# Casts of wo behind the second tile's exponentials, last output copies first and through the tail buffers, the first x block in two pairs of tiles, x stores moved

## The chip, the cores and the metric

The kernel runs on one core of a Trainium2 chip. The metric is the device time of one execution in microseconds (us). The kernel before was run three times: 1636.6, 1637.58 and 1639.58 us, so its median is 1637.58 us. The engines are called as the profile calls them: PE (matmuls), ACT (ScalarE), DVE (VectorE), POOL (GpSimd) and SP (the queue that issues most transfers).

## The reference

A layer norm without weights, a linear attention A on the normalised rows, and a gated feed-forward network B on the same rows, whose product is added to the input:

```python
x = A_x                                   # 1 x 2048 x 576
xn = _layernorm(x)
qkv = xn @ wqkv                           # 32 heads of 18
pq, pk = per-head q @ w_phi, k @ w_phi
phi_q = concat(softmax(pq), softmax(-pq)) # and phi_k likewise
kv = einsum("bhsf,bhsd->bhfd", phi_k, v); z = sum of phi_k over s
o = (phi_q @ kv) / (phi_q . z + 1e-6)
s = o @ wo
g = silu((silu(xn @ w_gate) * (xn @ w_up)) @ w_down)   # 576 -> 4608 -> 576
out = x + s * g
```

## The kernel before, in words

**Stages.** All matmuls take float32 values in split form: a rounded high part and a remainder (`split`: an ACT copy and a DVE subtraction, L58 and L59). First the rows are loaded in blocks of 512 (four tiles `xn` of 128 rows), normalised, transposed on PE and split into the resident tiles `X` (`norm_stats`, `norm_block`, to about 75 us). Then come the k and v products, softmaxes and sums of the attention (the kv stage, to about 229 us), then the q stage (to about 486 us): eight steps of two `q_tile`s (softmax features of q), `numer` (their product with the summed k and v) and `project` (the product with `wo`, held as `WOH` and `WOL`). `project` fills a PSUM tile `ps` of 128x288 with 15 matmuls (L614), ACT copies it to `so` (L619) and stores it to `s_dram`. From 512.6 us on runs the feed-forward network (FFN), to the end.

**FFN.** `w_gate` and `w_up` are cut into 36 blocks of 128 columns. Five of them ("early", `early_tile`, PSUM `pe`, ACT silu L119, DVE product L122) are worked off between the matmuls of the attention and straight ahead of the FFN; their result goes to `h_dram`. The other 31 are units that `gate_up_weights` fetches: a load `ld` (L676), four POOL subtractions into `ts` and `ld` (L694 to L697), splits into `w`, stores of the split weights to `w_dram` for the second half of the rows, and one load `wt` from `t_dram` (L692). A unit is seven products of seven matmuls each into the PSUM banks `px` (two buffers), `py`, `pw` and one half of `pd`; between its products ACT copies `px` into `py` (L761) and takes snapshots `s` of `px` (L736), which PE's next product into the same bank waits for. The down products (`pd`, L832) follow as fill-in from the second pair of blocks on; their weights are `dw`, made from the rows `rt`, `rb` or `acc` and POOL's differences `td` (L917 to L924).

**Tails.** The last 64 of the 576 rows of each `w_gate` and `w_up` block don't fill a matmul, so they are prepared apart, by `tails(n)` (L541 to L554), eight times for four blocks each: a load into `tl` (two buffers, L544), four POOL subtractions in `tl` (L546 to L549), an ACT cast into `th` (one buffer, L550), a DVE subtraction (L551), and twelve stores to `t_dram` issued by POOL (eight of `th`, four of `tl`, L554). A unit's `wt` load reads what its tail has stored. `tl` and `th` lie in the pool `qk` of the q stage.

**What sets the order.** The program is written once; a scheduler orders each engine's queue from priorities and estimated times. `issue_after` adds an edge within one engine. Buffers of a pool are handed out in the order in which the program asks for them: who asks later for the same slot waits for the earlier user. Each engine works through its queue in the order that results. In the source the tails are asked for after all steps of the q stage, each behind one of the q tiles' last products (`last_e`). `keep_x` (L301) stores three `X` tiles to `a_dram`; `split_wo` is asked for after the first two q tiles and stands behind `read[-1]`, DVE's last subtraction of the second one.

Of the kernel before, what the change touches and what calls it, by code (L numbers as in the profile page):

```python
# [9 lines left out]
F32 = mybir.dt.float32  # L10
F32R = mybir.dt.float32r
AF = mybir.ActivationFunctionType
ALU = mybir.AluOpType
# [4 lines left out]
P = 128  # L18
NT = S // P
BT = 512  # L20
# [3 lines left out]
HALF = D // 2  # L24
# [22 lines left out]
def gated_hedgehog_kernel(ctx: ExitStack, tc, x, w_qk, w_v, w_phi, wo, w_gu, w_tail, w_down, ident_in, mask_in, out):  # L47
# [65 lines left out]
    def early_tile(f, i, parts, js=(0, 1), banks=None):  # L113
# [10 lines left out]
        return last  # L124

    with ExitStack() as att:
        const = att.enter_context(tc.tile_pool(name="const", bufs=1))
# [8 lines left out]
        with ExitStack() as wst:  # L136
# [4 lines left out]
            with ExitStack() as pst:  # L141
# [17 lines left out]

                def norm_stats(bs, xns):  # L160
                    t = slice(4 * bs[0], 4 * bs[-1] + 4)
                    for i, xn in zip(range(t.start, t.stop), xns):
                        for k in range(2):
                            nc.vector.bn_stats(stats[:, i, k, :], xn[:, k * HALF:(k + 1) * HALF])
# [8 lines left out]
                    return nc.vector.scalar_tensor_tensor(q, mv[:, t, 0], -1.0, r, op0=ALU.mult, op1=ALU.mult)  # L173

                def norm_block(b, xns):
                    for n, (i, xn) in enumerate(zip(range(4 * b, 4 * b + 4), xns)):
                        if n % 2:
                            nc.scalar.activation(xn[:, 0:D], xn[:, 0:D], AF.Identity, bias=rt[:, i:i + 1],
                                                 scale=rs[:, i:i + 1])
                        else:  # L180
                            nc.vector.tensor_scalar(xn[:, 0:D], xn[:, 0:D], mv[:, i, 0:1], rs[:, i:i + 1],
                                                    op0=ALU.subtract, op1=ALU.mult)
                        for k in range(2):
                            nc.gpsimd.tensor_copy(xn[:, D + k * P:D + (k + 1) * P].rearrange("p (j n) -> p j n", j=4),
                                                  xn[:, 512 + 32 * k:544 + 32 * k].unsqueeze(1).to_broadcast([P, 4, 32]))
                    i, j = divmod(b, 2)
                    dst = XB[i][2 * j:2 * j + 2]
                    for c in range(3):
                        ps = pps.tile([P, 2, BT], F32, name="tp", bufs=3)
                        for m in range(2):  # L190
                            o = (2 * c + m) * P if c < 2 else D + m * P
                            for n in range(4):
                                nc.tensor.transpose(ps[:, m, n * P:(n + 1) * P], xns[n][:, o:o + P], ident)
                        if c < 2:
                            nc.scalar.copy(dst[c][:, 0:2], ps)
                            nc.vector.tensor_sub(dst[c][:, 3:5], ps, dst[c][:, 0:2])
                            continue
                        xr = prep.tile([P, 2, BT], F32, name="xr", bufs=1)
                        for m in range(2):
                            nc.scalar.copy(dst[m][:, 2], ps[:, m])  # L200
                        nc.scalar.copy(xr, ps)
                        for m in range(2):
                            nc.gpsimd.tensor_sub(dst[m][32:64, 2], xr[32:64, m], dst[m][32:64, 2])
                            nc.scalar.dma_start(x_dram[i, :, :, 2 * j + m].rearrange("s p n -> p s n"),
                                                xr[:, m].rearrange("p (s n) -> p s n", s=4))

                def load_fold(m):
# [46 lines left out]
                wq = load_fold(1)  # L254
                norm_stats([0, 1], xns)
                norm_block(0, xns[0:4])
# [16 lines left out]
            def softmax_parts(ps, e):  # L273
# [7 lines left out]
                for s in range(2):  # L281
                    nc.scalar.activation(e[:, s * D:(s + 1) * D], e[:, s * D:(s + 1) * D], AF.Exp,
                                         scale=1.0 if s == 0 else -1.0)
# [4 lines left out]
            kk_pool, read = kk, []  # L288

# [29 lines left out]
            def sum_parts(k):  # L319
                r = raws[k]  # L320
                lo = los[k] = kk.tile([P, 4, 2, P], F32R, name="slo", bufs=1)
                for a in (2, 0):
# [5 lines left out]
                    nc.sync.dma_start(sum_dram[k // 4, :, j, k % 4, 0:3], hi.bitcast(F32))  # L328
                    nc.sync.dma_start(sum_dram[k // 4, :, j, k % 4, 3:5], lo[:, j].bitcast(F32))

# [97 lines left out]
            for p in range(8):  # L428
# [93 lines left out]
        with ExitStack() as qst:  # L522
# [75 lines left out]
            def project(b, oh, ol, last):  # L598
                for j in range(QS // P):
# [3 lines left out]
                    for i in range(2):  # L603
# [8 lines left out]
                        for g, (o, w) in enumerate(GROUPS):  # L612
                            for a, bw in ((oh, WOH), (oh, WOL), (ol, WOH)):
                                nc.tensor.matmul(ps[:, 0:HALF], a[0:w, g, jc], bw[0:w, g, n], start=k == 0,  # L614
                                                 stop=k == 3 * NG - 1)
                                k += 1
                        so = qk.tile([P, HALF], F32, name="so", bufs=2)
                        with tc.high_priority() if last else ExitStack():
                            nc.scalar.copy(so, ps[:, 0:HALF])  # L619
                        nc.scalar.dma_start(s_dram[r0:r0 + P, n], so)  # L620
# [408 lines left out]
    early_tile(EARLY - 1, 0, parts)  # L1029
    ready = [gate_up_weights(*todo.pop(0))]  # L1030
    est.close()
# [74 lines left out]
```

## Time and profile before

| | |
|---|---|
| median of the runs | 1637.58 us (1636.6 to 1639.58) |
| the profiled execution | 1638.38 us, its span 1636.6 us, 25198 instructions |
| mean granted TensorE clock | 0.998 |
| PE busy | 1604.0 us, 98% of the span, 9385 matmuls |
| DVE, ACT, POOL busy | 1168.5, 721.9, 653.3 us |
| first FFN matmul | at 512.60 us |
| tails in the trace | first cast at 251.2, last at 420.2 us; stores from 253.0 to 430.3 us |

A row of the timeline gives the start, the duration, engine, line, operation, out<-in and count of a run of like instructions; in brackets stands the idle time of the engine ahead of it and what ended it. A row of the groups gives minimum, median and maximum of the duration of one instruction in ns. A row of the table by windows gives the window, its length and for each engine the busy time with the number of instructions, then the granted clock of PE, the share of the DMA engines and GB/s. A row of PE's waits gives who waited for what, the sum in us, how often, and the longest. A row of the DMA issues gives the transfer, its queue, count, size, and the median us from issue to landing.

### The profile page before, as it was taken

Reading aid. Unit: us, or ns where it says so; the run is one execution under the profiler, and the core shown is the slowest. Engines: PE = TensorE matmul, PEld = TensorE weight load, DVE = VectorE, ACT = ScalarE, POOL = GpSimd, SP = SyncE. Lnnn points to the kernel's source line nnn. Section 1 sums busy time; section 2 is a strip of 40 time slices with the busy share of each in tenths; the row PEclk is TensorE's granted clock in tenths of the full one; section 3 lists DMA queues with packets and bytes.
Section 4 is the critical chain, followed back from the end, with each engine's and each line's share of the span. In section 5 each row is a group of like instructions: output and inputs, shape, how many; then the busy total and the mean of one; then the engine's idle time right before and its main releaser. Section 6 shows DMA issues by size and latency. Waiting matters only on the chain.

```text
span 1636.6 us, 25198 instructions
## 1 busy us (share of the span) xinstructions
PE 1604.0 (98%) x9385; PEld 1429.7 (87%) x9385; DVE 1168.5 (71%) x1721; ACT 721.9 (44%) x1391; POOL 653.3 (40%) x699
## 2 busy tenths in 40 slices
PE   6999998999999999999999999999999999999998
PEld 5899997999978888888888888888888888888887
DVE  7677768899952678778777778825666766666578
ACT  5533345444432554544444544455433433333334
POOL 3485661333212455455545355313233324133132
PEclk9999999999999999999999999999999999999999
DMA  9622243334248545555554554684454655555444
GB/s 286 206 80 78 85 134 117 117 103 126 67 144 306 184 165 175 179 178 168 177 180 165 175 192 152 224 296 150 136 162 135 199 184 170 172 179 185 140 115 174
DMA packets 121741, 268.46 MB, mean 164 GB/s; under 512 B 12787, under 2 KB 53363, under 8 KB 119827
## 3 DMA queue, kind: packets, MB, share of 16 engines
q1 hardware_dynamic: 106652, 246.49, 45.9%
q0 software_dynamic: 3072, 11.02, 2.4%
q10 hardware_dynamic: 11894, 9.35, 1.8%
q8 instruction: 74, 1.21, 0.3%
q14 instruction: 49, 0.39, 0.1%
HBM read 167.19 MB, written 99.61 MB: 163 GB/s over the span
## 4 chain that ended last, share of the span: by engine, by line
PE 90%; DMA 4%; DVE 3%; POOL 1%; issue 1%; ACT 1%; SPq 0%; ACTq 0%; POOLq 0%; DVEq 0%
PE px L707 24%; PE pd L832 24%; PE pw L707 12%; PE py L707 6%; PE p L92 6%; PE pe L92 5%; PE p L614 4%; PE po L594 2%; PE kvp L294 2%; PE vx L382 1%; PE pt L588 1%; DMA xn<-in_A_x 1%; PE vw L382 1%; DMA s_dram<-so 1%; DMA sraw<-in_A_w_v 1%
## 5 line engine op out<-in xcount | busy, mean ns | idle before, releaser
L832 PEld LDWEIGHTS pd<-dw,hh 128*128 128x128 f32 x3048 | 432.4, 188 | 26.4 <-DVE dw L59 1.7
L832 PE MATMUL pd<-dw,hh 128*128 128x288 f32 x3048 | 448.5, 297 | 4.3 <-DVE dw L59 1.5
L707 PE MATMUL px<-X,w 128*128 128x512 f32 x1488 | 384.3, 393 | 0.0
L707 PEld LDWEIGHTS px<-X,w 128*128 128x128 f32 x1488 | 270.6, 188 | 51.8 <-ACT s L736 2.0
L707 PE MATMUL pw<-X,w 128*128 128x512 f32 x732 | 188.7, 393 | 0.0
L707 PEld LDWEIGHTS pw<-X,w 128*128 128x128 f32 x732 | 137.0, 188 | 30.5
L741 DVE TENSOR_TENSOR s<-pw,s 128x512 f32<-128x512 f32 x124 | 85.1, 688 | 100.0 <-ACT s L736 89.2
L957 DVE TENSOR_TENSOR acc<-pd,acc 128x576 f32<-128x576 f32 x128 | 96.2, 752 | 83.8 <-PE pd L832 83.6
L736 ACT COPY s<-px 128x512 f32<-128x512 f32 x124 | 72.6, 585 | 157.2 <-PE px L707 157.2
L92 PE MATMUL pe<-X,wh 128*128 128x512 f32 (+1 forms) x380 | 121.8, 401 | 5.8 <-ACT h L119 2.9
L59 DVE TENSOR_TENSOR hh<-ha,hh 128x512 fp32r<-128x512 f32 x140 | 111.5, 823 | 20.7 <-ACT hh L58 19.1
L58 ACT CAST hh<-ha 128x512 fp32r<-128x512 f32 x140 | 82.7, 619 | 92.4 <-PE pd L832 73.5
L929 POOL TENSOR_TENSOR hb<-hb 128x512 f32<-128x512 f32 x34 | 47.0, 1381 | 168.6 <-DVE hb L753 161.4
L59 DVE TENSOR_TENSOR w<-ld,w 128x512 fp32r<-128x512 f32 (+1 forms) x93 | 77.2, 832 | 35.7 <-ACT w L58 34.5
L707 PE MATMUL px<-X,wt 96*128 96x512 f32 x248 | 97.9, 395 | 0.0
L707 PE MATMUL py<-X,w 128*128 128x512 f32 x372 | 96.5, 394 | 0.0
L916 POOL TENSOR_TENSOR h<-ha,hb 128x512 f32<-128x512 f32 x34 | 44.3, 1302 | 126.8 <-DVE ha L757 88.6
L942 POOL TENSOR_TENSOR ha<-ha 128x512 f32<-128x512 f32 x34 | 52.6, 1564 | 103.5 <-DVE hh L59 103.5
L58 ACT CAST w<-ld 128x512 fp32r<-128x512 f32 (+1 forms) x93 | 51.0, 549 | 89.6 <-POOL ld L697 56.8
L92 PEld LDWEIGHTS pe<-X,wh 128*128 128x128 f32 (+1 forms) x380 | 70.0, 189 | 21.7 <-ACT h L119 3.4
L761 ACT COPY py<-px 128x512 f32<-128x512 f32 x62 | 35.5, 572 | 102.7 <-PE px L707 80.8
L707 PEld LDWEIGHTS py<-X,w 128*128 128x128 f32 x372 | 66.7, 188 | 11.2
(262 smaller groups left out, 3199.0 us busy)
## 6 DMA issues: line engine op xcount, KB each, us to landing
w_dram<-w SPq DMA_DIRECT2D x90, 512.0 KB, 2.9
w<-w_dram SPq DMA_DIRECT2D x90, 512.0 KB, 4.5
wt<-t_dram SPq DMA_DIRECT2D x61, 336.0 KB, 3.7
ld<-in_B_w_gu SPq DMA_DIRECT2D x31, 512.0 KB, 4.5
X<-sum_dram SPq DMA_DIRECT2D x8, 1280.0 KB, 11.1
rt<-in_B_w_down SPq DMA_DIRECT2D x33, 288.0 KB, 3.1
rb<-in_B_w_down SPq DMA_DIRECT2D x33, 288.0 KB, 4.7
w_dram<-w SPq DMA_DIRECT2D x30, 256.0 KB, 2.1
```

The costliest lines, as they stand in the source:

```text
L58: nc.scalar.copy(hi, src)
L59: nc.vector.tensor_sub(lo, src, hi)
L92: last = nc.tensor.matmul(ps, l, r, start=n == 0, stop=n == len(pairs) - 1)
L614: nc.tensor.matmul(ps[:, 0:HALF], a[0:w, g, jc], bw[0:w, g, n], start=k == 0, stop=k == 3 * NG - 1)
L707: nc.tensor.matmul(ps, l, r, start=first and n == 0, stop=last and n == len(mm) - 1, skip_group_check=True)
L736: nc.scalar.copy(t, ps)
L741: nc.vector.tensor_add(t, ps, t)
L832: nc.tensor.matmul(ps, l, r, start=first and n == 0 and m == 0, stop=n == len(hs) - 1 and m == 2, skip_group_check=True)
L916: sub(s, g["h"][0][0], g["h"][0][1])
L929: nc.gpsimd.tensor_add(a21, a21, g["h"][1][1])
L942: sub(a12, a12, g["h"][0][0])
L957: nc.vector.tensor_add(a2, pd[:, :, 0:HALF], a2)
```

## The change

The first block of x is normalised and transposed in two pairs of tiles, and the next block's statistics stand behind the first block's last subtraction on DVE (`rest`) instead of behind its statistics. The stores of `keep_x` are issued behind the last store of that step's sums (`done`). The casts of `wo` stand behind the second tile's last exponential on ACT (`exps[-1]`), and the third `wo` buffer is a slot of `e` instead of `ez`. In the last step's second half (`last and i`) the output copies go to slots of `tl`, and the first unit's loads and weights (`gate_up_weights`) are issued behind the last output copy.

```diff
-                def norm_stats(bs, xns):
-                    t = slice(4 * bs[0], 4 * bs[-1] + 4)
+                def norm_stats(t, xns):
...
+                def turn(ps, c, ns, xns):
+                    for m in range(2):
+                        o = (2 * c + m) * P if c < 2 else D + m * P
+                        for n in ns:
+                            nc.tensor.transpose(ps[:, m, n * P:(n + 1) * P], xns[n][:, o:o + P], ident)
...
-                chain = norm_stats([2], xns[0:4])
-                norm_block(2, xns[0:4])
+                tps = [pps.tile([P, 2, BT], F32, name="tp", bufs=3) for _ in range(3)]
+                for n in (0, 2):
+                    norm_stats(slice(8 + n, 10 + n), xns[n:n + 2])
+                    norm_tiles(slice(8 + n, 10 + n), xns[n:n + 2])
+                    for c in range(3):
+                        turn(tps[c], c, (n, n + 1), xns)
+                rest = norm_block(2, xns[0:4], tps)
                 first_weights = [early_weights(0)]
-                with tc.issue_after(chain.ins):
-                    norm_stats([3], xns[4:8])
+                with tc.issue_after(rest.ins):
+                    norm_stats(slice(12, 16), xns[4:8])
...
-                sum_parts(order[p - 1])
+                done = sum_parts(order[p - 1])
                 load_stack(order[p])
                 if p == 3:
-                    keep_x()
+                    with tc.issue_after(done.ins):
+                        keep_x()
...
-                   qk.tile([P, 2, D], F32, name="ez", bufs=1)]
+                   qk.tile([P, 2 * D], F32, name="e", bufs=4).rearrange("p (a n) -> p a n", a=2)]
...
             def split_wo():
-                with tc.issue_after(read[-1].ins):
+                with tc.issue_after(exps[-1].ins):
...
-                        so = qk.tile([P, HALF], F32, name="so", bufs=2)
+                        if last and i:
+                            so = qk.tile([P, 7, P], F32, name="tl", bufs=2).rearrange("p a n -> p (a n)")[:, 0:HALF]
+                        else:
+                            so = qk.tile([P, HALF], F32, name="so", bufs=2)
                         with tc.high_priority() if last else ExitStack():
-                            nc.scalar.copy(so, ps[:, 0:HALF])
+                            outs.append(nc.scalar.copy(so, ps[:, 0:HALF]))
...
-    ready = [gate_up_weights(*todo.pop(0))]
+    with tc.issue_after(outs[-1].ins):
+        ready = [gate_up_weights(*todo.pop(0))]
```

The change has its effect through the order of the queues. On ACT, at the start of the q stage (exponentials L282 of the kernel before, L298 of the changed one; L58 the casts of `wo` out of the buffers `oh`, `ol` and `ez` or `e`), the kernel before has:

```order
L282 ACTIVATE e<-e 128x576 x2
L58 CAST WOH<-oh 126x1152
L58 CAST WOH<-ol 126x1152
L58 CAST WOH<-ez 72x576
L550 CAST th<-tl 128x896
L282 ACTIVATE e<-e 128x576
```

And the changed kernel, at the same place:

```order
L119 ACT_TABLE_LOAD
L119 ACTIVATE h<-pe 128x512
L298 ACT_TABLE_LOAD
L298 ACTIVATE e<-e 128x576 x2
L58 CAST WOH<-oh 126x1152
L58 CAST WOH<-ol 126x1152
L58 CAST WOH<-e 72x576
```

The three casts have moved behind the second tile's two exponentials, and the cast of the first tail (L550) has left this place.

On ACT, from the early tiles' silus to the first snapshots of the FFN, the kernel before has (L119 an early tile's silu, L761 the copy of `px` into `py`, L736 a snapshot):

```order
L119 ACTIVATE h<-pe 128x512
L62 CAST wh<-raw 128x768
L58 CAST w_5391<-ld 128x256
L119 ACTIVATE h<-pe 128x512 x4
L761 COPY py<-px 128x512
L58 CAST dw<-acc 128x288
L58 CAST dw<-td 128x288 x2
L58 CAST w_5383<-ts 128x2x256
L736 COPY s<-px 128x512
```

The changed kernel (L569 is its cast of a tail, L783 its copy of `px` into `py`, L758 its snapshot):

```order
L119 ACTIVATE h<-pe 128x512
L569 CAST th<-tl 128x896
L58 CAST w_5398<-ld 128x256
L119 ACTIVATE h<-pe 128x512 x3
L569 CAST th<-tl 128x896
L783 COPY py<-px 128x512
L58 CAST w_5390<-ts 128x2x256
L58 CAST w_5394<-ld 128x2x256
L770 ACTIVATE py<-py 128x512
L569 CAST th<-tl 128x896 x6
L758 COPY s<-px 128x512
```

All eight casts of the tails now stand here, the last six of them in one row ahead of the first snapshot; none is left in the q stage.

On POOL, from the last two tails to the FFN's first differences, the kernel before has (L546 to L549 a tail's subtractions, L554 its stores, L694 and L695 a unit's):

```order
L546 TENSOR_TENSOR tl<-tl 128x128
L547 TENSOR_TENSOR tl<-tl 128x128
L548 TENSOR_TENSOR tl<-tl 128x128
L549 TENSOR_TENSOR tl<-tl 128x128
L554 DMA t_dram<-th 32x896 x8
L554 DMA t_dram<-tl 32x896 x4
L694 TENSOR_TENSOR ts<-ld 128x256
L695 TENSOR_TENSOR ts<-ld,ts 128x256
```

The changed kernel, from the second tail's stores (L573) to the third's, with L565 to L568 as a tail's subtractions and L716 to L718 as those of a unit:

```order
L573 DMA t_dram<-th 32x896 x8
L573 DMA t_dram<-tl 32x896 x4
L565 TENSOR_TENSOR tl<-tl 128x128
L716 TENSOR_TENSOR ts<-ld 128x256
L566 TENSOR_TENSOR tl<-tl 128x128
L567 TENSOR_TENSOR tl<-tl 128x128
L717 TENSOR_TENSOR ts<-ld,ts 128x256
L568 TENSOR_TENSOR tl<-tl 128x128
L718 TENSOR_TENSOR ld<-ld 128x256
L573 DMA t_dram<-th 32x896 x8
L573 DMA t_dram<-tl 32x896 x4
```

The third tail's subtractions are mixed with those of a unit's weights. After it five more tails follow on POOL, each as four subtractions, eight stores and four stores, and only then the first differences `td` of the down weights. On DVE the last six subtractions of the tails stand in one row ahead of the first `dw`; on SP the last five loads of `tl` stand in one row behind two loads `ld` and ahead of the loads of `acc`, `rt` and `rb`. On PE the order of the products changes as well: the seven matmuls into `px` that need the first snapshot are numbers 51 to 57 of the FFN, and the third unit's first product into `px` starts with number 72 (with number 100 before, behind two whole units).

More of the change, by code (lines that the diff above doesn't have):

```diff
@@ L124, in early_tile @@
         return last
+    outs = []
     with ExitStack() as att:
@@ L172, in norm_stats, with norm_tiles @@
                     nc.vector.scalar_tensor_tensor(r, q, 1.5, r, op0=ALU.add, op1=ALU.mult)
-                    return nc.vector.scalar_tensor_tensor(q, mv[:, t, 0], -1.0, r, op0=ALU.mult, op1=ALU.mult)
-                def norm_block(b, xns):
-                    for n, (i, xn) in enumerate(zip(range(4 * b, 4 * b + 4), xns)):
+                    nc.vector.scalar_tensor_tensor(q, mv[:, t, 0], -1.0, r, op0=ALU.mult, op1=ALU.mult)
+                def norm_tiles(t, xns):
+                    for n, (i, xn) in enumerate(zip(range(t.start, t.stop), xns)):
                         if n % 2:
@@ L185, in norm_block @@
                                                   xn[:, 512 + 32 * k:544 + 32 * k].unsqueeze(1).to_broadcast([P, 4, 32]))
+                def turn(ps, c, ns, xns):
[3 more added lines that the diff above has]
+                            nc.tensor.transpose(ps[:, m, n * P:(n + 1) * P], xns[n][:, o:o + P], ident)
+                def norm_block(b, xns, tps=None):
+                    if not tps:
+                        norm_tiles(slice(4 * b, 4 * b + 4), xns)
                     i, j = divmod(b, 2)
@@ L188, in norm_block @@
                     for c in range(3):
[L189 to L193, printed above, removed]
+                        if tps:
+                            ps = tps[c]
+                        else:
+                            ps = pps.tile([P, 2, BT], F32, name="tp", bufs=3)
+                            turn(ps, c, range(4), xns)
                         if c < 2:
                             nc.scalar.copy(dst[c][:, 0:2], ps)
-                            nc.vector.tensor_sub(dst[c][:, 3:5], ps, dst[c][:, 0:2])
+                            rest = nc.vector.tensor_sub(dst[c][:, 3:5], ps, dst[c][:, 0:2])
                             continue
@@ L205, in norm_block @@
                                                 xr[:, m].rearrange("p (s n) -> p s n", s=4))
+                    return rest
                 def load_fold(m):
@@ L254, in gated_hedgehog_kernel @@
                 wq = load_fold(1)
-                norm_stats([0, 1], xns)
+                norm_stats(slice(0, 8), xns)
                 norm_block(0, xns[0:4])
@@ L281, in softmax_parts @@
                 for s in range(2):
-                    nc.scalar.activation(e[:, s * D:(s + 1) * D], e[:, s * D:(s + 1) * D], AF.Exp,
-                                         scale=1.0 if s == 0 else -1.0)
+                    last = nc.scalar.activation(e[:, s * D:(s + 1) * D], e[:, s * D:(s + 1) * D], AF.Exp,
+                                                scale=1.0 if s == 0 else -1.0)
+                exps.append(last)
                 sm = kk_pool.tile([P, 2 * H], F32, name="sm")
@@ L286, in softmax_parts @@
                 return sm
-            kk_pool, read = kk, []
+            kk_pool, read, exps = kk, [], []
             def kv_step(n, phi, v):
@@ L328, in sum_parts @@
                     nc.sync.dma_start(sum_dram[k // 4, :, j, k % 4, 0:3], hi.bitcast(F32))
-                    nc.sync.dma_start(sum_dram[k // 4, :, j, k % 4, 3:5], lo[:, j].bitcast(F32))
+                    done = nc.sync.dma_start(sum_dram[k // 4, :, j, k % 4, 3:5], lo[:, j].bitcast(F32))
+                return done
             V1, V2 = slice(D + HALF, 2 * D), slice(D, D + HALF)
```

1 line of the change is left out of this document (added).

## The prediction

> **What bounds the kernel now.** I read the page first, then the engines by windows, PE's waits in the two stages that the change touches, and the timelines of the tails and of the FFN's opening.
>
> ```profile
> span 1636.6 us, 25198 instructions
> PE 1604.0 (98%) x9385; PEld 1429.7 (87%) x9385; DVE 1168.5 (71%) x1721; ACT 721.9 (44%) x1391; POOL 653.3 (40%) x699
> ```
>
> PE is busy in all but 33 us of the span, and the change removes no matmul. So it can gain only out of those 33 us, while it can lose as much as it makes PE wait. The windows, with PE in the second column behind the length, show where PE's idle time lies:
>
> ```profile
> 0.00:42.00 42.00, 27.27 (x149) 23.13 (x150) 30.78 (x74) 23.83 (x33) 15.97 (x32) 0.96 0.91 286
> 97.00:225.00 128.00, 128.00 (x990) 125.74 (x989) 93.20 (x119) 46.70 (x120) 86.30 (x86) 1.00 0.26 84
> 240.00:275.00 35.00, 30.84 (x169) 26.10 (x169) 29.28 (x44) 19.99 (x24) 7.59 (x16) 1.00 0.53 167
> 320.00:457.00 137.00, 137.00 (x948) 126.83 (x947) 126.49 (x198) 60.70 (x109) 42.20 (x87) 1.00 0.33 100
> 457.00:486.00 29.00, 27.55 (x162) 22.81 (x161) 12.10 (x21) 12.00 (x24) 5.40 (x7) 1.00 0.39 130
> ```
>
> 14.7 us lie in the first window (loads and the first norm), 4.2 us at the start of the q stage, 1.5 us at its end. Between 320 and 457 us PE has no gap, although most of the tails run there: their work costs nothing where it stands now.
>
> **The q stage: casts of wo and output copies.** PE waits there for these:
>
> ```profile
> PE pe L92 <- ACT h L119: 2.1, 3, 1.2
> PE pe L92 <- DVE h L122: 1.6, 1, 1.6
> PE p L92 <- DVE e L279: 1.4, 1, 1.4
> PE p L614 <- ACT so L619: 1.2, 1, 1.2
> ```
>
> And ACT's timeline shows why some of them are there: the cast of `oh` keeps the queue for 3.99 us until its load has landed, that of `ol` for 2.04 us, and the second tile's exponential (252.04) stands behind all of them.
>
> ```profile
> 244.86 1.16 ACT L58 CAST WOH<-oh 126x1152 fp32r<-126x1152 f32 x1 [3.99 <-DMA oh<-in_A_wo]
> 248.05 1.16 ACT L58 CAST WOH<-ol 126x1152 fp32r<-126x1152 f32 x1 [2.04 <-DMA ol<-in_A_wo]
> 252.04 0.68 ACT L282 ACTIVATE e<-e 128x576 f32<-128x576 f32 x1
> 253.46 1.28 ACT L119 ACT_TABLE_LOAD   x1
> ```
>
> In the new order the exponentials pass ahead. The four waits sum to 6.3 us, the most that the edits can give here; 0 is the least, since the silus and DVE's steps keep their own chains. I take half, 3 us. The two extra buffers for the copies remove the wait of 1.2 us on `so`, which is within those 3 us. That the casts come later costs nothing: `WOH` is first read by `project` one step on, with two q tiles of PE work between; without that cover the three casts would be some 3 us.
>
> **First block and x stores.**
>
> ```profile
> 10.44 5.36 PE L193 MATMUL tp<-ident,xn 128*128 128x128 f32 x24 [10.44 <-DVE xn L181]
> 15.64 0.82 DVE L164 BATCH_NORM_STATS2 stats<-xn 128x6 f32<-128x288 f32 x2 [4.76 <-DMA xn<-in_A_x]
> 16.38 2.34 DVE L196 TENSOR_TENSOR X<-tp,X 128x1024 fp32r<-128x1024 f32 x2
> 17.64 5.91 PE L221 MATMUL tp<-PHI,wst 126*128 126x126 f32 x36 [1.83 <-DVE X L196]
> a_dram<-X SPq DMA_DIRECT2D x3, 1280.0 KB, 5.6
> ```
>
> With the pairs, half of the 24 transposes (2.7 of 5.36 us) are done before the last tile is normalised, and with `rest` DVE no longer waits for the next block's tile (4.76 us) ahead of the subtractions at 16.38, for which the fold waits 1.83 us. Together the fold can come forward by 2.7 + 1.8 = 4.5 us at most. Against it: a second chain of small DVE steps, and two more table loads on ACT (1.28 us each, 2.6 us). And PE stops next at 33.47 (row below) for the next block's norm, whose statistics now start later: what PE gains ahead it may lose there. Bounds -4 to +3 us; I take -1, nearer to nothing, since the wait at 33.47 is already there. The three `a_dram` stores (5.6 us to landing each) leave the opening, where the DMA share is 0.91, for a stage in which it is 0.26 and PE has no gap in 128 us: SP's queue has slack there, bounds -1 to +2, taken as 0.
>
> **The tails: from hidden to the FFN's opening.** The copies of the last outputs ask for both slots of `tl` ahead of the tails, so that the tails get them only when these copies are stored, after the stage's end (486 us in the last window above). The orders show the outcome: all eight tails stand at the FFN's opening. What one costs:
>
> ```profile
> 249.21 0.46 POOL L546 TENSOR_TENSOR tl<-tl 128x128 f32<-128x128 f32 x1 [10.16 <-DMA h_dram<-h]
> 251.12 0.47 POOL L546 TENSOR_TENSOR tl<-tl 128x128 f32<-128x128 f32 x1
> L550 ACT CAST th<-tl x8: 923/944/951, 251.2 to 420.2; 128x896 fp32r<-128x896 f32 x8
> 294.11 3.96 POOL L554 DMA_DIRECT2D t_dram<-th  x8
> 298.06 2.00 POOL L554 DMA_DIRECT2D t_dram<-tl  x4
> t_dram<-th POOLq DMA_DIRECT2D x64, 112.0 KB, 3.4
> t_dram<-tl POOLq DMA_DIRECT2D x32, 112.0 KB, 2.5
> ```
>
> From one tail's first subtraction to the next one's are 1.91 us for four subtractions; then 0.94 the cast, 3.96 and 2.00 the issue of twelve stores. With one `th` and POOL in order, a tail can't start its cast before POOL has issued the stores of the one before and done its own subtractions, so a round is 1.91 + 0.94 + 3.96 + 2.00 = 8.8 us, about 9.0 with the handovers. The other loop, cast, stores of `th` and their landing, is 0.94 + 3.96 + 3.4 = 8.3 us, a little shorter. In the kernel before these casts lay between 251 and 420 us, where PE had its own work. In the new order PE needs a snapshot that stands behind six of them. Where PE gets to by then:
>
> ```profile
> 512.60 0.40 PE L745 MATMUL py<-X,w 128*128 128x512 f32 x1
> ...
> 535.44 1.54 PE L707 MATMUL px<-X,w 128*128 128x512 f32 x6
> ...
> 540.20 0.53 PE L832 MATMUL pd<-dw,hh 128*128 128x288 f32 x2 [1.10 <-DVE hh L59]
> 542.23 1.33 PE L832 MATMUL pd<-dw,hh 128*128 128x288 f32 x8 [1.50 <-DVE dw L59]
> 509.51 0.60 ACT L119 ACTIVATE h<-pe 128x512 f32<-128x512 f32 x1 [5.96 <-PE pe L92]
> 519.13 3.01 SPq L687 DMA_DIRECT2D w_dram<-w x2
> 522.23 0.55 SPq L676 DMA_DIRECT2D ld<-in_B_w_gu  x1
> ld<-in_B_w_gu SPq DMA_DIRECT2D x31, 512.0 KB, 4.5
> ```
>
> From 512.60 to 535.44 PE does 99 matmuls, 0.231 us each. So PE is through the 50 matmuls ahead of the stalled product at 512.6 + 11.5 = 524.1 us. On ACT the second tail's cast stands behind the last silu (509.51 + 0.60), so it starts at 510.2 and POOL has issued its stores at 510.2 + 0.94 + 5.96 = 517.1. The third tail's subtractions are mixed on POOL with those of a unit whose `ld` stands in SP's queue behind stores of `w` that wait for PE to free and ACT to fill buffers, as the `ld` at 522.23 stands behind the stores at 519.13 now. With that time, 522.2 + 4.5 landing + some 3.2 for the mixed subtractions puts the third cast at 529.9. Five rounds of 9.0 more put the eighth at 574.9, and the snapshot at about 576.4: PE has stood for 52 us.
>
> Then it runs a few products and stops again: the third unit's first `px` product needs the first pair's silus and sums, whose ACT queue has `dw` casts ahead that wait for POOL's `td`, and POOL is still storing the last tail.
>
> ```profile
> rb<-in_B_w_down SPq DMA_DIRECT2D x33, 288.0 KB, 4.7
> 518.81 0.95 POOL L917 TENSOR_TENSOR td<-rb,rt 128x288 f32<-128x288 f32 x1 [1.42 <-DMA rb<-in_B_w_down]
> ```
>
> Counted from the eighth cast: 0.94 + 5.96 of stores + 2.5 landing (the buffers for `rb` and `td` lie where `tl` and `th` were) + 4.7 for `rb` + three differences of at most 0.95 + about 2 for the casts and silu = 19 us, so 594. Without any stall PE would be there 28 matmuls (6.5 us) earlier in its order than before, at 535.4 - 6.5 = 528.9. The loss is 594 - 529 = 65 us; the 2.6 us of waits that PE has at 540 to 542 now fall away, and about as much is lost by slow matmuls after the stalls:
>
> ```profile
> 33.47 2.80 PE L193 MATMUL tp<-ident,xn 128*128 128x128 f32 x18 [0.92 <-DVE xn L181]
> ```
>
> PE's first 24 transposes, after 10.44 us of idling, took 5.36 us, or 0.22 each; 18 later ones took 2.80, or 0.16, and the granted clock of the first window is 0.96 against 1.00 elsewhere. So a restart after a long idle costs some 1.5 us, two of them 3. The Trainium skill, in "TensorE: Matmul & The Clock Gate", section "Part 1: The HAM clock gate (the "warmup" mystery)", has the clock halved after an idle window of about 3.4 us until about 3.4 us of work have passed, which would be 1.7 us a restart; the trace agrees as far as its transposes go.
>
> Sum against the profiled execution: 1638.4 (the profiled execution, its span of 1636.6 and 1.8 around it) - 3 (q stage) - 1 (first block) + 0 (x stores) + 65 (tails) = 1699.4. The median, 1637.6, lies 0.8 us below the profiled time, so 1698.6 us.
>
> **The rivals.** First, the same stall without the wait on `ld`: if that load is issued ahead of the stores, the third cast follows the second tail's stores directly, at 517.1 + 3.2 = 520.3, 9.6 us earlier, and the time is 1689. The row at 522.23 speaks against it, the shorter PE order of the second unit for it. Chance 0.22. Second, longer rounds: in the trace before, a load of `tl` took 6.7 us to land; with two buffers a load can start only when the tail before last has landed its stores. 2.5 + 6.7 = 9.2 us after a round's end is just over a round, so it may set the pace, and with the DMA queues full of `w` stores a round may be 11 us:
>
> ```profile
> tl<-in_B_w_tail SPq DMA_DIRECT2D x8, 256.0 KB, 6.7
> ```
>
> Six rounds of 2 us more give 1711. Chance 0.14. Third, on the other side: the tails stay hidden and only the gains in the q stage show. The mechanism would be that the twelve stores of a tail hold POOL only because they wait now, and go out at once when POOL is free. The six rounds between 510.2 and 524.1 would then have to take 2.3 us each; that is the point from which it decides. 1637.6 - 3 - 1 = 1633.6. Against it: the eight stores at 294.11 and four at 298.06 follow each other without a gap at 0.50 us each, and their row names no releaser. Chance 0.04. Fourth, the order on the chip does the same but the q stage and the first block give nothing: 1702.6, inside the forecast. That the moved tails cost little because PE finds other work is excluded by its one queue; what I can have overlooked there gets 0.03 for about 1640.
>
> **How the numbers follow.** The forecast itself, 0.57, spans 1692 to 1708: the third cast within 5 us, the q stage 0 to 6.3, the first block -4 to +3. The first rival adds the lower end, down to 1682 with a second stall of 10 instead of 19 us; the second adds the upper, up to 1714. Outside lie the two last cases and the far ends of the first two, some 0.15. A measurement of this kernel can tell about 0.2%, or 3.3 us, from no change: faster 0.04, same 0.03, slower 0.93.
>
> **What would show it.** In the changed profile the casts of `th` lie after 485 us, the last six some 9 us apart, with POOL's stores filling the time between; PE has one wait of about 50 us from near 524 for ACT's snapshot and a second of about 10 to 15 us; the span beyond 600 us is as long as before. A third cast near 520 shows the first rival, rounds of 11 us the second. The q stage's waits for `so` and `e` are gone. The prediction is wrong if PE's longest wait is under 20 us, or if the tails' casts are found under the q stage.

## The result and the profile after

The changed kernel takes 1711.95 us (median of 4 runs, 1711.36 to 1712.64) against 1638.12 us before (median of four runs, one more than in the table further up): ratio 1.0449, 95% interval 1.0436 to 1.0462, 73.8 us slower. The forecast was 1698.6 us with a range of 1682 to 1714. The page after:

```profile
span 1709.9 us, 25191 instructions
PE 1615.5 (94%) x9385; PEld 1437.1 (84%) x9385; DVE 1170.8 (68%) x1727; ACT 725.0 (42%) x1394; POOL 652.6 (38%) x699
```

The number of matmuls is the same. Of the 73.3 us by which the span has grown, PE idles 61.8 us more (94.4 against 32.6), and is busy 11.5 us longer with the same work. The windows show where both lie (PE busy first, the granted clock third from the end):

```profile
240.00:275.00 35.00, 31.70 (x167) 26.59 (x165) 30.89 (x46) 18.07 (x23) 0.95 (x1) 1.00 0.45 141
510.00:525.00 15.00, 12.09 (x41) 9.30 (x40) 2.48 (x3) 2.54 (x4) 6.39 (x13) 0.77 1.00 357
525.00:580.00 55.00, 5.64 (x25) 4.30 (x23) 6.16 (x6) 5.79 (x7) 39.93 (x82) 0.59 0.66 199
580.00:620.00 40.00, 28.89 (x104) 22.31 (x105) 20.23 (x28) 15.51 (x30) 26.25 (x36) 0.76 0.60 193
620.00:890.00 270.00, 269.26 (x1496) 238.80 (x1495) 213.81 (x303) 137.25 (x275) 137.27 (x133) 1.00 0.51 174
```

PE does next to nothing from 530 to 583 us, at a time when POOL is busy for 40 of 55 us, mostly with issuing stores. From 620 to 890 us PE is busy but for 0.7 us, at a granted clock of 1.00. PE's timeline at the opening of the FFN:

```profile
513.00 0.40 PE L767 MATMUL py<-X,w 128*128 128x512 f32 x1
...
518.13 0.79 PE L729 MATMUL px<-X,wt 96*128 96x512 f32 x1 [2.91 <-DMA wt<-t_dram]
...
530.25 0.39 PE L729 MATMUL pd<-X,wt 96*128 96x512 f32 x1
583.46 2.93 PE L729 MATMUL px<-X,w 128*128 128x512 f32 x6 [52.82 <-ACT s L758]
586.19 0.63 PE L729 MATMUL px<-X,wt 96*128 96x512 f32 x1
587.59 2.93 PE L729 MATMUL px<-X,w 128*128 128x512 f32 x6 [0.77 <-ACT s L758]
590.31 0.63 PE L729 MATMUL px<-X,wt 96*128 96x512 f32 x1
590.74 2.37 PE L729 MATMUL pw<-X,w 128*128 128x512 f32 x6
592.94 0.40 PE L729 MATMUL pw<-X,wt 96*128 96x512 f32 x1
598.09 5.16 PE L729 MATMUL px<-X,w 128*128 128x512 f32 x12 [4.75 <-DVE hb L775]
```

The wait of 52.8 us is the one that the prediction puts at 52. What ACT does meanwhile is the tails' casts; the second one, three of the last six, and the snapshot behind them:

```profile
510.42 0.93 ACT L569 CAST th<-tl 128x896 fp32r<-128x896 f32 x1
...
535.60 0.94 ACT L569 CAST th<-tl 128x896 fp32r<-128x896 f32 x1 [8.88 <-POOL tl L568]
544.82 0.94 ACT L569 CAST th<-tl 128x896 fp32r<-128x896 f32 x1 [8.29 <-POOL tl L568]
...
581.99 0.94 ACT L569 CAST th<-tl 128x896 fp32r<-128x896 f32 x1 [8.55 <-DMA t_dram<-tl]
582.83 0.58 ACT L758 COPY s<-px 128x512 f32<-128x512 f32 x1
```

From 535.60 to 581.99 are five rounds of 9.28 us. POOL in one of them:

```profile
542.85 0.47 POOL L565 TENSOR_TENSOR tl<-tl 128x128 f32<-128x128 f32 x1
...
544.34 0.45 POOL L568 TENSOR_TENSOR tl<-tl 128x128 f32<-128x128 f32 x1
546.05 4.04 POOL L573 DMA_DIRECT2D t_dram<-th  x8 [1.26 <-ACT th L569]
550.08 1.98 POOL L573 DMA_DIRECT2D t_dram<-tl  x4
552.08 0.47 POOL L565 TENSOR_TENSOR tl<-tl 128x128 f32<-128x128 f32 x1
```

POOL waits only 1.26 of 9.23 us, for the cast; the rest is 1.94 us of subtractions and 6.02 us of issuing stores (the rows with L573).

### The profile page after: what moved, and what is told of

Read it like the earlier page. It is cut to its first block, busy times and chain, and to the rows that moved or that the text cites. A ratio compares the mean times of both kernels' runs of the same rounds, so it can differ in the third digit from the quotient of the medians.

```text
span 1709.9 us, 25191 instructions
## 1 busy us (share of the span) xinstructions
PE 1615.5 (94%) x9385; PEld 1437.1 (84%) x9385; DVE 1170.8 (68%) x1727; ACT 725.0 (42%) x1394; POOL 652.6 (38%) x699
## 4 chain that ended last, share of the span: by engine, by line
PE 62%; POOL 3%; DMA 2%; DVE 2%; issue 1%; ACT 1%; SPq 0%; POOLq 0%; DVEq 0%
PE px L729 22%; PE pd L854 22%; PE pw L729 11%; PE py L729 6%; POOL t_dram L573 2%; PE pe L92 1%; DMA rb<-in_B_w_down 0%; DMA wt<-t_dram 0%; DMA t_dram<-tl 0%; DVE hh L59 0%; DVE acc L826 0%; ACT th L569 0%; DVE w L59 0%; DMA ld<-in_B_w_gu 0%; SPq L709 0%
## 5 line engine op out<-in xcount | busy, mean ns | idle before, releaser
L729 PE MATMUL px<-X,w 128*128 128x512 f32 x1488 | 390.4, 398 | 59.5 <-ACT s L758 54.8
L729 PEld LDWEIGHTS px<-X,w 128*128 128x128 f32 x1488 | 274.2, 191 | 114.1 <-ACT s L758 58.4
L716 POOL TENSOR_TENSOR ts<-ld 128x256 f32<-128x256 f32 x31 | 26.9, 868 | 327.9 <-DMA ld<-in_B_w_gu 253.4
L758 ACT COPY s<-px 128x512 f32<-128x512 f32 x124 | 72.7, 586 | 156.5 <-PE px L729 156.4
L58 ACT CAST hh<-ha 128x512 fp32r<-128x512 f32 x140 | 82.7, 619 | 92.0 <-PE pd L854 72.9
L58 ACT CAST w<-ld 128x512 fp32r<-128x512 f32 (+1 forms) x93 | 51.0, 549 | 87.8 <-POOL ld L719 53.2
L783 ACT COPY py<-px 128x512 f32<-128x512 f32 x62 | 35.4, 572 | 106.2 <-PE px L729 88.0
## 6 DMA issues: line engine op xcount, KB each, us to landing
X<-sum_dram SPq DMA_DIRECT2D x8, 1280.0 KB, 11.3
```

Of the source, the lines that this page charges most:

```text
L58: nc.scalar.copy(hi, src)
L729: nc.tensor.matmul(ps, l, r, start=first and n == 0, stop=last and n == len(mm) - 1, skip_group_check=True)
L758: nc.scalar.copy(t, ps)
L783: nc.scalar.copy(yp, xp)
```

## The experiments

All times are medians, with the ratio to runs of the kernel before on the same chip (1638.26 us beside the first four runs, 1638.55 beside the next four, 1639.02 beside the last four).

**Who asks first.** One edit to the changed kernel: the tails are asked for ahead of the last projection.

```diff
             for n in range(S // QS + 1):
...
+                if n == S // QS:
+                    for t in range(TAILS):
+                        with tc.issue_after(last_e[3 * t // 2 + 2].ins):
+                            tails(t)
                 if n > 0:
                     project(order[n - 1], *om, n == S // QS)
...
-            for n in range(TAILS):
-                with tc.issue_after(last_e[3 * n // 2 + 2].ins):
-                    tails(n)
```

> The changed kernel, with one thing moved: the eight tails are asked for ahead of the last projection, so that the output copies get the tail buffers after them. Same instructions. Theory (the copies took the tail buffers, so all tails slid behind them): the casts of th return to 250 to 430 us, PE's wait of 52.8 us for the snapshot is gone, and the time falls by about 73 us to 1634 to 1642. Rival (the loss comes from the other edits: later casts of wo, weights of the first unit behind the last copy, x stores): it stays above 1700 us.

Measured: 1643.29 us, ratio 1.0037 (1.0022 to 1.0052). The tails' casts are back under the q stage:

```profile
L569 ACT CAST th<-tl x8: 924/944/949, 251.9 to 422.8; 128x896 fp32r<-128x896 f32 x8
```

68.7 of the 73.8 us go with this edit, which moves only the place of a request. That is the cause. But the rest is not faster than before, as it was to be, but 5 us slower, and the time lies 1.3 us above the expected range.

**Copies in so.** The changed kernel with the last copies in `so`:

```diff
-                        if last and i:
-                            so = qk.tile([P, 7, P], F32, name="tl", bufs=2).rearrange("p a n -> p (a n)")[:, 0:HALF]
-                        else:
-                            so = qk.tile([P, HALF], F32, name="so", bufs=2)
+                        so = qk.tile([P, HALF], F32, name="so", bufs=2)
```

> The changed kernel with the last output copies back in the two buffers of so; all other edits stay. Theory: no tail moves, 1634 to 1640 us, and against the run above the wait of ACT or PE for so may come back, 0 to 1.2 us. By the terms of the prediction (3 us in the q stage, 1 in the first block) it is 1634; by the profile after, in which the first FFN matmul comes at 513.0 instead of 512.6 us, these terms gave nothing and it is 1638. Rival as above: over 1700.

Measured: 1647.52 us, ratio 1.0059 (1.0039 to 1.0078). The stall is gone here too, so the rival is refuted. But the time lies 7.5 us above the theory's range, and its median 4 us above that of the first run instead of at most 1.2 (the two intervals overlap). In the profiled executions the FFN opens at 516.3 instead of 511.9 us. The buffers of `so` don't explain that: ACT's third copy waits 3.25 us for a store, but it waits 3.29 us in the kernel before as well, and PE doesn't wait for a copy in this run. The difference stands earlier, in the q stage, where PE waits 3.17 us for an early tile's silu at 257.54 us and 1.33 us for `e` at 259.37; in the first run neither wait is there. What puts them there is not shown.

**The tail buffers alone.** The kernel before with the opposite edit (the `if last and i` branch of the diff above, nothing else).

> The kernel before with one edit alone: the last output copies go to the tail buffers. Theory: the whole loss comes from this edit, 1708 to 1715 us, with tails in rounds of 9.2 us behind 490 us. Rival (several edits share the loss): under 1690.

Measured: 1706.05 us, ratio 1.0411 (1.0396 to 1.0427), PE waits 45.8 us for the snapshot and 5.0 for `wt`. 67.8 us come from this edit alone. The time is 2 us under the theory's lower end and far above the rival's.

**Stores on SP.** The changed kernel with `nc.gpsimd.dma_start(t_dram...)` turned into `nc.sync.dma_start(t_dram...)`.

> The changed kernel with the twelve stores of each tail issued by SP instead of POOL. Theory (the round of 9.2 us is subtractions, cast and POOL's 12 issues of 0.5 us): SP issues at 0.32 to 0.43 us and POOL no longer holds the next subtractions, so a round falls to 5.5 to 7 us and the time by 13 to 25 us, to 1687 to 1699. Rival (the round is set by transfers: the landing of the stores out of the one th, or the load of tl into two buffers): the round stays near 9 us and the time at 1709 to 1715.

Measured: 1699.23 us, ratio 1.0368 (1.0354 to 1.0383). The time is at the theory's upper end, but not for its reason: the rounds grew to 11.3 us instead of falling.

```profile
533.38 0.94 ACT L569 CAST th<-tl 128x896 fp32r<-128x896 f32 x1 [10.29 <-POOL tl L568]
539.83 0.42 SPq L563 DMA_DIRECT2D tl<-in_B_w_tail  x1
544.67 0.94 ACT L569 CAST th<-tl 128x896 fp32r<-128x896 f32 x1 [10.35 <-POOL tl L568]
```

SP's queue now holds the stores, from 534.34 to 539.79 us, and behind them the next load of `tl`, for which POOL's subtractions wait until 542.71. PE stands in other places (29.9 us for `X<-sum_dram`, which waits in the same queue), and when that wait begins, at 527.8 us, four tails have been cast instead of two. This run doesn't tell issue from transfer.

**Stores split.** The same question, without SP: eight of each tail's stores on ACT.

```diff
-                        nc.gpsimd.dma_start(t_dram[n, q, b], src[32 * q:32 * q + 32])
+                        (nc.scalar if b else nc.gpsimd).dma_start(t_dram[n, q, b], src[32 * q:32 * q + 32])
```

> The changed kernel with eight of each tail's twelve stores (the second copy of th, and tl) issued by ACT, four left on POOL; SP's queue as it was. Theory (the round of 9.2 us is 1.9 subtractions + 1.3 wait for the cast + 6.0 issue of stores on POOL): a round falls to 5.2 to 6.5 us, the eighth cast comes between 540 and 560 us instead of 582, and the time is 1665 to 1692. Rival (the round is set by landing of the stores and loads of tl, 2.7 + 3.9 us, not by issue): rounds of 7.7 us or more, and over 1695.

Measured: 1699.49 us, ratio 1.0371 (1.0356 to 1.0385).

```profile
543.83 8.66 ACTq L573 DMA_DIRECT2D t_dram<-tl  x4
...
560.69 0.94 ACT L569 CAST th<-tl 128x896 fp32r<-128x896 f32 x1 [6.45 <-DMA t_dram<-tl]
...
568.24 0.94 ACT L569 CAST th<-tl 128x896 fp32r<-128x896 f32 x1 [6.61 <-DMA t_dram<-tl]
```

The shortest rounds are 7.6 and 7.9 us, the three before them 9.2 to 11.8, and the eighth cast comes at 568. So the time is the rival's, and something sets the pace soon after POOL's issue has gone down. What it is stays open. In the two shortest rounds the profile puts the cast's wait down to a store of `tl`, as the rival has it. But the edit also puts eight stores into the queue in which the next cast stands: in the round from 541.01 to 552.81, ACT's four stores of `tl` alone took 8.66 us to issue (the first row), while POOL had ended the subtractions at 547.5. So 1.6 us, by which the shortest round lies under 9.2, is the least that POOL's issue was worth, not its measure.

**The other edits one at a time, on the kernel before.** The casts of `wo` (`issue_after(exps[-1].ins)` and the slot of `e`):

> The kernel before with the casts of wo behind the second tile's last exponential and the third buffer a slot of e, nothing else. Prediction's term: 3 us faster in the q stage, most 6.3, so 1632 to 1637.6 us. Rival (as the profile after suggests: fillers take the place of the waits or the waits move to e): within 1 us of before.

The pairs of tiles (`tps`, `turn`, and the next block's statistics behind `rest`):

> The kernel before with the first x block in two pairs of tiles and the next block's statistics behind rest, nothing else. Prediction's term: 1 us faster, bounds -4 to +3. Rival, from the profile after (PE waits 14.2 instead of 11.4 us for xn in the opening and its clock there is 0.92 instead of 0.96): 1 to 3 us slower.

The x stores behind `done`:

> The kernel before with the three stores of x issued behind the last store of the step's sums, nothing else. Prediction's term: 0, bounds -1 to +2 us. Rival: in the profile after PE waits in the opening are as long and DMA share falls from 0.91 to 0.84; if those stores delayed loads that PE waits for, 1 to 3 us faster.

The first unit behind the last copy (`issue_after(outs[-1].ins)`):

> The kernel before with the first unit's loads and weights issued behind the last output copy, nothing else. No term in the prediction: 0, since ACT's casts of w then no longer stand between the last copies (so copies up to 2 us earlier) but PE has early tiles to work on. Bounds -1.5 to +1 us.

| alone | median us | ratio, 95% interval |
|---|---|---|
| casts of wo | 1640.23 | 1.0013 (1.0003 to 1.0022) |
| pairs of tiles | 1641.35 | 1.0018 (1.0009 to 1.0027) |
| x stores | 1637.78 | 0.9996 (0.9987 to 1.0004) |
| first weights | 1638.16 | 0.9999 (0.9990 to 1.0008) |

The two edits from which gains were forecast cost 2 and 3 us by their medians, 0.1 and 0.2%; the other two are within what can be told. For the pairs this is their rival; for the casts it is neither the theory nor the rival. What the casts do to the order, the profile shows (its execution took 1642.5 us, 2.3 us more than the run's median). ACT's queue is free of the waits for `oh` and `ol` as planned, but DVE's order has changed with it: the early tile's product `h` stands ahead of the first q tile's subtractions. The kernel before starts the last of these at 235.97, this run at 244.45:

```profile
235.97 0.76 DVE L279 TENSOR_TENSOR e<-p,m 128x576 f32<-128x576 f32 x1
```

```profile
242.39 0.69 DVE L122 TENSOR_TENSOR h<-pe,h 128x512 f32<-128x512 f32 x1 [5.86 <-PE pe L92]
...
244.45 0.76 DVE L279 TENSOR_TENSOR e<-p,m 128x576 f32<-128x576 f32 x1
```

So PE waits twice in 3 us, and in this execution it then runs slowly for some 3.4 us (the windows show the clock third from the end):

```profile
243.23 0.47 PE L92 MATMUL pe<-X,wh 128*128 128x512 f32 x1 [0.70 <-DVE h L122]
245.35 0.37 PE L92 MATMUL p<-QH,X 128*128 128x288 f32 x1 [1.65 <-DVE e L279]
```

```profile
244.00:248.00 4.00, 2.65 (x14) 2.68 (x15) 3.92 (x7) 1.15 (x2) 0.00 (x0) 0.80 0.84 258
248.00:252.00 4.00, 4.00 (x21) 3.78 (x21) 2.94 (x4) 0.00 (x0) 1.03 (x3) 0.78 1.00 336
```

The same two waits stand in the changed kernel, where the clock stays at 1.00 in these windows. So the slow stretch does not always follow them (see the last section).

For the pairs, the fold comes forward, from 17.64 to 16.99 us, but PE gets to the next block's transposes only to wait longer (4.16 us instead of 0.92) and then to work at a clock of 0.50:

```profile
16.99 4.28 PE L231 MATMUL tp<-PHI,wst 126*128 126x126 f32 x36 [0.65 <-DVE X L205]
...
35.45 5.24 PE L190 MATMUL tp<-ident,xn 128*128 128x128 f32 x24 [4.16 <-DVE xn L180]
```

```profile
35.00:40.00 5.00, 4.55 (x22) 4.58 (x23) 4.10 (x7) 2.30 (x4) 3.24 (x7) 0.50 0.71 224
```

This wait has grown by 3.2 us: PE came 1.2 us earlier, and the norm ended 2.0 us later. On ACT the norm's square root now stands behind a silu and two table loads (the first at 25.43), at 29.47 instead of 25.23 us; 2.0 of these 4.2 us reach the norm's end.

```profile
25.23 0.20 ACT L168 ACTIVATE rs<-mv 128x4 f32<-128x4 f32 x1 [0.85 <-DVE mv L167]
```

```profile
26.73 0.60 ACT L119 ACTIVATE h<-pe 128x512 f32<-128x512 f32 x1
...
28.18 1.28 ACT L167 ACT_TABLE_LOAD   x1
29.47 0.20 ACT L167 ACTIVATE rs<-mv 128x4 f32<-128x4 f32 x1
```

**The parts that cost nothing, together.** The kernel before with the x stores, the first weights, the copies in the tail buffers, and the tails asked for ahead of the last projection (the diff of the first run); without the pairs and without the later casts.

> The kernel before with the parts that cost nothing alone: x stores moved, first weights behind the last output copy, output copies in the tail buffers, but the tails asked for ahead of the last projection. Not in it: the pairs of tiles and the later casts of wo. By the single runs: x stores -0.8, first weights -0.4, the wait for so (1.2 us) gone: 1635 to 1638.5 us, at most 0.2% faster than before. Rival (the early copies themselves cost something at the FFN's opening, as the wait of 4.9 us there in the first run of this series): 1640 or more.

Measured: 1636.71 us, ratio 0.9988 (0.9979 to 0.9997): the smallest median of all, but only 2.3 us or 0.12% below the kernel before beside it. In its profile the FFN opens at 508.90 us instead of 512.60, PE waits nowhere between 450 and 512 us, and the wait for `so` is gone.

**And with the casts of wo.** The same plus that edit.

> As the run above, with the casts of wo behind the second tile's last exponential added, so that against the first run of this series only the pairs of tiles are missing. If the terms add: the run above + 2 us, so 1637 to 1641, and 3 us below the first run of this series (1643.3). Rival (wo and the early copies act on each other at the FFN's opening): 1642 to 1645, and the pairs cost nothing here.

Measured: 1643.35 us, ratio 1.0028 (1.0018 to 1.0038). The terms don't add: the casts of `wo` cost 2 us alone and 6.6 us here. The FFN opens 2.8 us later than in the run without them (511.71), with the same two waits at the start of the q stage, and at 550 us PE meets a wait that the run without them has not:

```profile
550.31 2.93 PE L715 MATMUL px<-X,w 128*128 128x512 f32 x6 [3.76 <-ACT s L744]
```

The granted clock is 0.50 to 0.55 from 550 to 556 us behind it. The casts alone have a wait there too (3.04 us at 551.72), but the clock behind it stays at 1.00. In the profile of this run, and in that of the first of the series (511.92), the FFN opens a little earlier than in the kernel before (512.60), so all that these two lose is lost behind its opening. Why the snapshot comes late there is not shown.

Against the first run of the series (ratio 1.0037, intervals overlapping) the pairs cost little or nothing in this company: the rival of that expectation holds.

**PE kept busy.** The changed kernel with more matmuls ahead of the product that waits; they write into a half bank that nobody reads.

```diff
...
+            if opening == 1:
+                for _ in range(224):
+                    nc.tensor.matmul(zt[:, 1], w[0][3][:, 0], S4[0], start=True, stop=True)
```

> The changed kernel with 224 more matmuls ahead of the product that waits for the snapshot, into an unused half of the pd bank; they add no result. 224 x 0.231 = 51.7 us fill the wait of 52.8 us. Theory (after a long wait PE runs at half clock for some us): the stall ends at the same time, the 21 matmuls behind it take 0.23 instead of 0.43 us each, and the time falls by 3 to 5 us to 1707 to 1709. Rival (the slow matmuls have another cause, such as transfers): no change, 1711 to 1713, or later by what the added matmuls overrun.

Measured: 1710.03 us, ratio 1.0434 (1.0420 to 1.0448), 1.9 us less than the changed kernel, whose interval overlaps.

```profile
528.27 51.01 PE L799 MATMUL pd<-X,w 128*128 128x512 f32 x224
583.01 2.52 PE L729 MATMUL px<-X,w 128*128 128x512 f32 x6 [3.73 <-ACT s L758]
585.33 0.63 PE L729 MATMUL px<-X,wt 96*128 96x512 f32 x1
586.73 2.92 PE L729 MATMUL px<-X,w 128*128 128x512 f32 x6 [0.77 <-ACT s L758]
```

The filling ended 3.7 us too early, and the products behind it were slow again. So the run shows less than it was made for: behind a gap of 3.7 us matmuls are slow too (the granted clock is 1.00 to 583 us and 0.50 from 585 to 589); whether they vanish without a gap stays open.

## Why the prediction was right, point by point

**The mechanism and its place** are as forecast: all eight tails at the FFN's opening, PE standing for the first snapshot, a second wait after it, next to nothing behind 620 us. Two of the signs are not: the second wait is 4.75 us, not 10 to 15, and of the two waits in the q stage that were to go, only that for `so` is gone; PE still waits for `e`, 1.65 us at 245.25 and 0.95 at 256.49. That it is the order of the requests for `tl` was argued from the order of the queues; the first and third runs show it, from both sides (68.7 and 67.8 us).

**The number** is right by luck in part. 1711.95 us lies above the 1692 to 1708 that the forecast's own terms span; the stated range holds it only because the second rival, whose longer rounds did not come, drew it out to 1714.

**The term of the tails** was 65 us, measured 68 to 69. Its pieces: the second tail's cast was put at 510.2 and came at 510.42. The third was put at 529.9 and came at 535.60; the `ld` that it had to wait for was issued behind the stores of `w`, as the forecast had it and the first rival had not, but at 527.8 instead of 522.2 us:

```profile
525.03 2.75 SPq L709 DMA_DIRECT2D w_dram<-w  x3
527.83 1.58 SPq L698 DMA_DIRECT2D ld<-in_B_w_gu  x2
```

The likely reason is that PE itself was late to free the `w` buffers: it waited 2.91 us for `wt` at 518.13 (not in the sum) and ran slowly after it. Rounds were put at 9.0 and took 9.28. PE's wait was 52.8 against 52 us only because PE came later to it, 530.6 against 524.1, as the snapshot did; that these two agree is luck as well. The third unit's first product was put at 594 and came at 598.1, 16 instead of 19 us behind the eighth cast.

**Slow matmuls** were put at 3 us for two restarts, and this size was wrong: the step that failed is "a restart after a long idle costs some 1.5 us, two of them 3". By the rows of the profile after: 20 matmuls from 518.13 to 525.64 take 7.5 instead of 4.6 us, the 21 from 583.46 to 593.34 take 9.1 (without the wait of 0.77) instead of 4.9, the 13 from 598.09 take 5.2 instead of 3.0: some 9.3 us. PE restarts three times, not two, and the granted clock is 0.50 from 518 to 524, from 583 to 591 and from 597 to 601 us. The row from which the price was taken was also misread. By the rows of the kernel before, the 24 slow transposes ran while the clock was granted in full; it fell only after them:

```profile
10.00:15.00 5.00, 4.56 (x21) 4.29 (x22) 0.88 (x2) 3.22 (x4) 2.22 (x8) 1.00 1.05 259
15.00:20.00 5.00, 3.17 (x21) 2.93 (x20) 4.36 (x10) 2.84 (x5) 2.02 (x2) 0.89 0.89 337
20.00:25.00 5.00, 5.00 (x29) 4.71 (x29) 4.57 (x11) 3.34 (x5) 0.48 (x1) 0.77 0.91 240
```

So the trace does not bear out that the transposes show the clock's price; what slowed them is not shown.

**The small terms** were -3 (casts of `wo`) and -1 (pairs), together 4 us faster. Alone they measure about +2 and +3 us, and all edits but the displaced tails together +5. The steps that failed: "the four waits sum to 6.3 us ... I take half" looked at these waits alone, while the edit also changed DVE's and PE's order; and "what PE gains ahead it may lose there" was the right warning at the next block's norm, weighed too low: the wait at 33.47 grew from 0.92 to some 4 us and brought slow matmuls with it. In the changed kernel PE's waits from 225 to 490 us do fall by 3 us, from 6.3 to 3.3, but the FFN opens at 513.0 instead of 512.6 us, so this gain is lost elsewhere, 2.8 us of it in longer waits for the first norms (14.2 against 11.4 us). The x stores at 0 hold; the first weights, for which the prediction has no term, cost nothing either.

**How the 13 us divide** by which the forecast is low depends on the way of counting. By the runs it is 9 for the small terms (+5 instead of -4) and 4 for the tails with the slow matmuls, if the terms add; the runs with and without the casts show that they don't. By the trace of the changed kernel the FFN opens at 513.0 instead of 508.6, which is 4.4 us for the small terms; some 4 more are lost up to the third unit's first product, and some 4 behind it, in slow matmuls and in waits of 0.46 and 1.58 us at 607 and 615 that were to fall away.

**The rivals.** The first (no wait for `ld`) is out by the rows above. The second gave 1711 us, which is the measured time, but not its mechanism: rounds were 9.28, not 11 us. (It also counts six longer rounds where the forecast has five from the third cast on; five would give 1709.) Its warning that buffers and landing lie just under POOL's issue agrees with the two shortest rounds of the split stores, but isn't proven by them. The third, tails that stay hidden, would have needed rounds of 2.3 us. The fourth, in which the small edits give nothing (1702.6), is nearer to what these edits did than the forecast, but it has them at nothing where together they cost 5 us.

## What to carry to other kernels

A buffer name lent to another step is a place in a line: who asks first in program order gets it first, and everything that asks later slides behind the borrower's last use, with all its transfers. Here a wait of 1.2 us was removed by borrowing, at 68 us; asking for the tails first keeps that wait away without the price. Where a scheduler sets the order, read the new order of every engine that the moved step shares, not only of the one that was to be relieved.

## What the runs showed of the hardware that was not expected

- The same two waits of PE, 0.70 and 1.65 us within 3 us, stand at the start of the q stage in the changed kernel and in seven of the runs. In four of these eight (tails asked first, stores on SP, stores split, casts of `wo` alone) the granted clock then fell, to between 0.50 and 0.80 in the window from 244 to 248 us; in the other four it stayed at 1.00 up to 252 us. Where it fell with the casts of `wo` alone, the slow matmuls began some 1.2 us after PE had resumed. Waits of 1.19, 1.55 and 1.42 us some 5 us and more apart in the kernel before left it at 1.00. The Trainium skill, "TensorE: Matmul & The Clock Gate", section "Part 1: The HAM clock gate (the "warmup" mystery)", speaks of an idle window of about 3.4 us; here 2.35 us of waiting, broken by one matmul, sometimes sufficed and sometimes not, and what decides is not shown.
- POOL issues a store of 32x896 elements in 0.50 us, with no gap between twelve of them; the same stores cost SP 0.45 us each (3.57 for eight, 1.78 for four, in the run with the stores on SP). On ACT four took from 1.74 to 8.66 us, in the run with the stores split.
